# Turning results back on the vector engine, handing out stores and loads one by one, and reading transposed probabilities back on the scalar engine's queue

## The chip, the cores and the metric

The kernel runs on one core of a Trainium2 chip. The time is device microseconds from one launch, the median of several runs; a profile is one further execution, recorded by the hardware. The core has five engines that each work through their own list of instructions in order and wait for each other through semaphores: TensorE (PE), VectorE (DVE), ScalarE (ACT), GpSimd (POOL) and SyncE (SP). SP does no arithmetic here: it issues DMAs, in the order in which the program gives them.

## What is computed

Two blocks follow each other, for 8 batches, 576 rows and 512 columns:

```python
# attention, 8 heads of 64 columns, S = 576 rows
scores = scale * q @ k.T
kth    = the 32nd largest score of each row
attn   = softmax of the scores, those below kth left out
x      = attn @ v, heads side by side            # (8, 576, 512)
# mixer
u   = x + (x.T @ U @ V).T                        # rank 32, over the rows
out = u + relu(u @ w_ch1) @ w_ch2                # 512 -> 2048 -> 512
```

All tensors are float32 (parameters arrive in 64 bits and are narrowed on the chip).

## The kernel before

The work goes by *pairs* of heads (`g`, 32 of them, four to a batch) and, within a pair, by *chunks* of query rows (`t`): four of 128 rows that hold both heads side by side, and one of 64 rows per head, stacked. A *step* `n` is one chunk; 160 steps follow each other, and each step's code issues work of several chunks at different stages: scores of chunk n+1 (`scores`, L323), top-32 search of chunk n (`front`: MAX8 and MATCH_REPLACE8 on VectorE, L432 to L463, a fold of the row's two halves in `pair` with L390, L392, L393), masking (L488 on ScalarE, L491 on GpSimd) and exponential (L397) of chunk n or n-1, transposing of the probabilities of chunk n-1, and the product with v of chunk n-3 or so (`values`, L581, L585). The instructions are issued in the order in which the Python code calls them (a manual schedule); each engine runs its own in that order.

The probabilities must be transposed before the product with v. For most chunks (`shared`) VectorE does it in blocks of 32x32 (`blocks`, L518, into the buffer `y`), four DMAs on SP write `y` to DRAM (`away`, L524), and a fifth reads it back as `PT` (L528), so that the blocks land in their places. The last 64 columns are transposed on TensorE (L551) and copied by ScalarE (L552).

`load(g)` (L238) issues all loads of a pair on SP: for most pairs (`blocked`) 16 DMAs for q and k (L247, L252) and 5 for v (L276, L279, L280). `prep(g)` turns q and k with VectorE's 32x32 transpose (L293) at the end of chunk 1 of the pair before.

The MLP of a batch (`mlp`, L646) is a generator. It yields after each matmul, and `fill` (L748), called eight times in a step, takes as many matmuls from it as the ratio of the work asks for; so the MLP of one batch is spread over the attention of the next. The MLP has two parts by rows (320 and 256), each with 16 blocks of the first product (L656, a Relu on ScalarE, L668) and 4 column blocks of the second (L675). The result `oT` of a column block has columns in partitions. ScalarE copies it (L690), GpSimd adds u (L691), and it is *turned back*: `turned_back` (L696) makes a closure that `mlp` calls 13 matmuls later, or at once for the last block of a batch:

```python
                late.append(turned_back(b, chunks, lo, c, oT))
                yield w / C
        late.pop()()
```

For all batches but the last, the closure transposes with TensorE (L723, three or two transposes), copies with ScalarE (L725, L727) and stores with one or two DMAs (L729, L734). In the last batch all blocks but one are transposed by VectorE in 32x32 blocks (L705), and 12 or 8 DMAs (L710, L715) store the pieces where they belong. The last batch's MLP has no attention beside it.

Of the kernel before, what the change touches and what calls it, by code (L numbers as in the profile page):

```python
# [26 lines left out]
def kernel(  # L27
# [107 lines left out]
    def half(h):  # L135
        return slice(h * D, (h + 1) * D)
# [96 lines left out]

    raw, qkTs, S2s, uTs, XTs, dens = {}, {}, {}, {}, {}, {}
    probs, PTs, folds, fronts_of = {}, {}, {}, {}
    inverted = set()

    def load(g):  # L238
        b, h0 = g // NPAIR, 2 * (g % NPAIR)
        ld = loads.tile([P, 2 * S], F32, tag="ld", name="ld")  # L240
        if blocked(g):
            for i, src in enumerate((q, k)):
                for a in range(4):
                    ds = src[b, h0 + a // 2, :, a % 2 * BLK : (a % 2 + 1) * BLK]
                    to = ld[a * BLK : (a + 1) * BLK, i * S : (i + 1) * S]
                    lead = TAIL if i and a >= 2 else 0
                    nc.sync.dma_start(  # L247
                        to[:, lead : lead + MAIN].rearrange("i (t m d) -> i t m d", t=NT, d=BLK),
                        ds[0:MAIN].rearrange("(m i t) d -> i t m d", i=BLK, t=NT),
                    )  # L250
                    end = 0 if lead else MAIN
                    nc.sync.dma_start(  # L252
                        to[:, end : end + TAIL].rearrange("i (m d) -> i m d", d=BLK),
                        ds[MAIN:S].rearrange("(m i) d -> i m d", i=BLK),
                    )
            raw[g] = ld
        else:
            tiles = []
            ends = ld[:, 2 * MAIN : 2 * S].rearrange("p (h d) -> p h d", h=2)
            for j, src in enumerate((q, k)):  # L260
                t = ld[:, j * MAIN : (j + 1) * MAIN].rearrange("p (t h d) -> p t h d", t=NT, h=2)
                for i in range(2):
                    queue = nc.scalar if g == 0 and i else nc.sync
                    queue.dma_start(
                        t[:, :, i, :],
                        src[b, h0 + i, 0:MAIN, :].rearrange("(p t) d -> p t d", t=NT),
                    )
                tiles.append(t)
            for i, src in enumerate((q, k)):
                nc.sync.dma_start(  # L270
                    ends[half(i)], src[b, h0 : h0 + 2, MAIN:S, :].rearrange("h p d -> p h d")
                )
            raw[g] = tiles, ends
        va, vd, vt = (a[g % NV] for a in (vas, vds, vts))
        for i in range(2):
            nc.sync.dma_start(  # L276
                va[:, i], v[b, h0 + i, 0:MAIN, :].rearrange("(p t) d -> p t d", t=NT)
            )
            nc.sync.dma_start(vd[half(i), half(i)], v[b, h0 + i, MAIN:S, :])  # L279
        nc.sync.dma_start(vt[TAIL:P], v[b, h0 : h0 + 2, MAIN:S, :].rearrange("h p d -> p h d"))  # L280

    def blocked(g):

        return g > NPAIR
# [222 lines left out]
    def blocks(g, t):  # L509


        E2 = probs[g, t]
        PT = attn.tile([P, 2 * NT + 1, P], F32, tag="PT", name="PT")
        PTs[g, t] = PT
        y = attn.tile([P, 4, 2, NT, BLK], F32, tag="y", name="y", bufs=1)
        for h in (1, 0):
            a = h * (S + TAIL)
            nc.vector.transpose(  # L518
                y[:, :, h].rearrange("p r c j -> p c r j"),
                E2[:, a : a + MAIN].rearrange("p (c r j) -> p c r j", c=NT, r=4),  # L520
            )
        away = dram.tile([P, 4, 2 * P], F32, tag="away", name="away")
        for a in range(4):
            nc.sync.dma_start(  # L524
                away[:, a].rearrange("(r i) n -> i r n", r=4),
                y[a * BLK : (a + 1) * BLK].rearrange("i r h c j -> i r (h c j)"),
            )
        nc.sync.dma_start(  # L528
            PT[:, 0 : 2 * NT].rearrange("p a n -> p (a n)"), away.rearrange("p a n -> p (a n)")
        )  # L530

    def turns(g, t):

# [112 lines left out]
    def mlp(b):  # L646

        uT = uTs.pop(b)
        late = []
        for chunks, (lo, hi) in zip(PARTS, SPAN):  # L650
            w = hi - lo
            hTs = []
            for f in range(NF):
                ph = ps_m.tile([P, C], F32, tag="mm", name="mm")
                for cc in range(NC):
                    nc.tensor.matmul(  # L656
                        ph[:, 0:w],
                        lhsT=w1[:, cc, f * P : (f + 1) * P],
                        rhs=uT[:, cc, lo:hi],
                        start=(cc == 0),  # L660
                        stop=(cc == NC - 1),
                    )
                    if cc < NC - 1:
                        yield w / C
                if f % 2 == 0:
                    hT = mlpp.tile([P, 2, WIDE], F32, tag="hT", name="hT", bufs=HT)
                    hTs += [hT[:, 0], hT[:, 1]]
                nc.scalar.activation(hTs[f][:, 0:w], ph[:, 0:w], AF.Relu)  # L668
                if f == 4 and late:
                    late.pop()()  # L670
                yield w / C
            for c in range(NC):
                po = ps_m.tile([P, C], F32, tag="mm", name="mm")
                for f in range(NF):
# [4 lines left out]
                        start=(f == 0),  # L679
                        stop=(f == NF - 1),  # L680
                    )
                    if f == 12 and late:
                        late.pop()()
                    if f < NF - 1:
                        yield w / C
                oT = mlpp.tile([P, WIDE], F32, tag="oT", name="oT")
# [2 lines left out]
                else:  # L689
                    nc.scalar.copy(oT[:, 0:w], po[:, 0:w])  # L690
                    nc.gpsimd.tensor_tensor(oT[:, 0:w], oT[:, 0:w], uT[:, c, lo:hi], ALU.add)  # L691
                late.append(turned_back(b, chunks, lo, c, oT))
                yield w / C
        late.pop()()

    def turned_back(b, chunks, lo, c, oT):  # L696


        def run():
            cs = slice(c * P, (c + 1) * P)  # L700
            if b == B - 1 and (lo, c) != (SPAN[1][0], NC - 1):

                w = sum(rows(t) for t in chunks)
                ob = mlpp.tile([P, 3 * P], F32, tag="ob", name="ob", bufs=2)
                nc.vector.transpose(ob[:, 0:w], oT[:, 0:w])  # L705
                for a in range(4):
                    cs = slice(c * P + a * BLK, c * P + (a + 1) * BLK)
                    ba = ob[a * BLK : (a + 1) * BLK]
                    for t in chunks[0:2]:
                        nc.sync.dma_start(  # L710
                            out[b, 0:MAIN, cs].rearrange("(m i t) c -> t i m c", i=BLK, t=NT)[t],
                            ba[:, OFF[t] - lo : OFF[t] - lo + P].rearrange("i (m c) -> i m c", c=BLK),
                        )
                    if NT in chunks:
                        nc.sync.dma_start(  # L715
                            out[b, MAIN:S, cs].rearrange("(m i) c -> i m c", i=BLK),
                            ba[:, 2 * P : 2 * P + TAIL].rearrange("i (m c) -> i m c", c=BLK),
                        )
                return
            tp = ps_t.tile([P, 3, P], F32, tag="tp", name="tp")  # L720
            for i, t in enumerate(chunks):
                n = rows(t)
                nc.tensor.transpose(tp[0:n, i, :], oT[:, OFF[t] - lo : OFF[t] - lo + n], ident)  # L723
            ob = mlpp.tile([P, 3, P], F32, tag="ob", name="ob", bufs=2)
            nc.scalar.copy(ob[:, 0:2], tp[:, 0:2, :])  # L725
            if NT in chunks:
                nc.scalar.copy(ob[0:TAIL, 2], tp[0:TAIL, 2, :])  # L727
            t = chunks[0]
            nc.sync.dma_start(  # L729
                out[b, 0:MAIN, cs].rearrange("(p t) c -> p t c", t=NT)[:, t : t + 2, :],  # L730
                ob[:, 0:2],
            )
            if NT in chunks:
                nc.sync.dma_start(out[b, MAIN:S, cs], ob[0:TAIL, 2])  # L734

        return run

    MLP_WORK = 2 * NF * NC * S / C

# [5 lines left out]
    share = MLP_WORK / (NPAIR * SLOTS * (NT + SHORT))  # L745
    fillers, mixing, due = [], [], 0.0

    def fill(k=1):  # L748


        nonlocal due
        for _ in range(k):
            if passes:
                passes.pop(0)()
            if mixing and next(mixing[0], True):
                mixing.pop(0)
            due += share * (SHORT if t == NT else 1) * (EARLY if n <= 2 * ALONE + 2 else 1)
# [13 lines left out]
        if m % CH == NT:  # L771
            mixing.append(mixed(m // CH, 5, 1 if m < STEPS - 1 else 0))

    load(0)
    next_params(1)
    t = 0
    for _ in prep(0):
# [4 lines left out]
    for n in range(STEPS + 2):  # L782
        g, t = divmod(n, CH)
        if n < STEPS:
            if t == 0 and g + 1 < NP:
                load(g + 1)
            if t == 1 and g + 1 < NP:
                ready = prep(g + 1)
            fronts[n] = front(g, t)
            next(fronts[n])  # L790
# [79 lines left out]
        next(turning, None)  # L870
        if n > ALONE and (n - 1) % CH < NT:
            next(last, None)
        fill()
        next(turning, None)
        fill()
# [22 lines left out]
        fill(2)  # L898
    while mixing or fillers:
        fill()  # L900


# [29 lines left out]
```

## Time and profile before

| | |
|---|---|
| median of 3 runs | 1718.4 us (1717.51 to 1718.5) |
| the profiled execution | 1716.65 us, of which the span from first to last instruction is 1714.9 us |
| TensorE clock granted, mean | 0.970 |
| busy: TensorE matmul | 1613.5 us, 94% of the span |
| busy: VectorE | 1484.2 us, 87% |
| busy: ScalarE | 1023.3 us, 60% |
| busy: GpSimd | 944.9 us, 55% |
| DMA | 167.37 MB in 275837 packets, 98 GB/s; 173920 of the packets under 512 B |

A line of the profile names the source line, the engine, the operation and the program's names (written <- read). In the groups the count follows the x, then come the busy time in us and the mean in ns, then the time that the engine was idle before such an instruction, and what ended that wait. In a timeline the first number is the start in us. A float32 matmul appears as two records, a transpose as one. Matmuls overlap in TensorE's pipeline, so the mean of one is longer than the distance between two. A name with a q (SPq) is the engine's queue of instructions that it issues without computing, such as DMAs.

### The profile page before, as it was taken

To read this page: it belongs to the slowest core of one execution; us is meant where nothing else is said; L and a number is where in the kernel's file an instruction comes from. 1 tells how busy PE (TensorE), PEld (TensorE's weight loads), DVE (VectorE), ACT (ScalarE), POOL (GpSimd) and SP (SyncE) were. 2 spreads that over 40 slices of the span, in tenths; PEclk is the share of its full clock that TensorE was granted. 3 is DMA by queue.
4 is the path that set the end of the run, shared out by engine and by line. 5 is a ranking of instruction groups with operands and counts; after the bars stand their busy time and mean duration, and the time that the engine had idled before them with its cause. 6 is when DMAs were issued, how large, how long until landed. Compare 5 with 4: busy or idle time off the path is not lost.

```text
span 1714.9 us, 29637 instructions
## 1 busy us (share of the span) xinstructions
PE 1613.5 (94%) x9489; PEld 1219.8 (71%) x9489; DVE 1484.2 (87%) x4317; ACT 1023.3 (60%) x2582; POOL 944.9 (55%) x749
## 2 busy tenths in 40 slices
PE   4666799998999999999999999999999999999999
PEld 2444566787777877788677877788677877788777
DVE  7999989999999999999999999999999999992000
ACT  4888797665656556565656566565655566563100
POOL 4778578666555555565555555565555555552000
PEclk7777899999999999999999999999999999999999
DMA  3322322344444444444444444444444444432010
GB/s 87 95 84 84 84 78 61 77 123 122 108 112 112 117 117 106 112 116 114 115 109 111 119 112 108 114 113 114 111 108 120 118 108 114 106 93 71 3 16 13
DMA packets 275837, 167.37 MB, mean 98 GB/s; under 512 B 173920, under 2 KB 260192, under 8 KB 275680
## 3 DMA queue, kind: packets, MB, share of 16 engines
q1 hardware_dynamic: 274624, 165.20, 37.2%
q8 instruction: 75, 1.23, 0.3%
q14 instruction: 82, 0.67, 0.1%
q10 hardware_dynamic: 1056, 0.26, 0.1%
HBM read 101.42 MB, written 63.96 MB: 96 GB/s over the span
## 4 chain that ended last, share of the span: by engine, by line
PE 71%; DVE 19%; SPq 3%; ACT 2%; issue 2%; DMA 2%; POOL 1%; POOLq 0%; DVEq 0%; ACTq 0%
PE mm L656 27%; PE mm L675 21%; PE sc L323 8%; DVE upper L458 6%; PE O L585 6%; DVE m L463 6%; DVE first L446 2%; SPq L252 2%; PE tp L551 1%; PE O L571 1%; SPq L247 1%; PE up L631 1%; PE O L581 1%; PE tp L546 1%; DVE y L518 1%
## 5 line engine op out<-in xcount | busy, mean ns | idle before, releaser
L675 PE MATMUL mm<-hT,w 128*128 128x256 f32 (+1 forms) x2048 | 529.5, 407 | 0.0
L656 PE MATMUL mm<-uT,w 128*128 128x256 f32 (+1 forms) x2048 | 522.8, 407 | 0.0
L491 POOL TENSOR_TENSOR Ssb<-Ssb,E 128x576 f32<-128x576 f32 x271 | 379.2, 1417 | 246.2 <-ACT E L488 245.8
L656 PEld LDWEIGHTS mm<-uT,w 128*128 128x128 f32 x2048 | 380.0, 191 | 97.6 <-issue 2.6
L675 PEld LDWEIGHTS mm<-hT,w 128*128 128x128 f32 x2048 | 377.9, 191 | 93.0 <-issue 2.9
L463 DVE MAX8 m<-upper 128x8 f32<-128x304 f32 (+1 forms) x864 | 407.7, 508 | 3.6
L458 DVE MATCH_REPLACE8 upper<-m,upper 128x304 f32<-128x304 f32 (+1 forms) x576 | 285.7, 502 | 0.0
L390 POOL TENSOR_TENSOR lower<-Ssb 128x576 uint32<-128x576 uint32 (+1 forms) x135 | 174.3, 1291 | 147.2 <-ACT Ssb L351 51.0
L393 POOL TENSOR_TENSOR lower<-lower,upper 128x576 uint32<-128x576 uint32 (+1 forms) x135 | 174.3, 1291 | 112.2 <-DVE upper L392 104.7
L397 ACT ACTIVATE Ssb<-Ssb,nmax 128x576 f32<-128x576 f32 x286 | 221.5, 777 | 15.3 <-POOL Ssb L468 9.3
L668 ACT ACTIVATE hT<-mm 128x320 f32<-128x320 f32 (+1 forms) x256 | 105.1, 410 | 192.9 <-PE mm L656 191.0
L323 PE MATMUL sc<-qkT 64*128 64x288 f32 x1334 | 211.7, 441 | 8.6 <-ACT Ssb L358 7.8
L488 ACT ACTIVATE E<-Ssb,least 128x576 f32<-128x576 f32 x271 | 198.0, 769 | 5.2
L323 PEld LDWEIGHTS sc<-qkT 64*128 64x128 f32 x1334 | 116.3, 183 | 63.8 <-issue 24.2
L585 PE MATMUL O<-PT,va 128*64 128x128 f32 x2048 | 144.5, 285 | 3.3 <-DMA PT<-away 3.2
L518 DVE STREAM_TRANSPOSE y<-Ssb 128x512 f32<-128x512 f32 x208 | 134.5, 682 | 14.8 <-ACT Ssb L397 14.7
L351 ACT COPY Ssb<-sc 128x576 f32<-128x576 f32 x216 | 127.5, 643 | 32.6 <-PE sc L323 31.0
L688 DVE TENSOR_TENSOR oT<-uT,mm 128x320 f32<-128x320 f32 (+1 forms) x8 | 3.6, 454 | 144.5 <-PE mm L675 144.5
L585 PEld LDWEIGHTS O<-PT,va 128*64 128x64 f32 x2048 | 113.2, 140 | 19.7 <-DMA PT<-away 3.9
L432 DVE MAX8 upper<-lower 128x8 f32<-128x288 f32 x243 | 97.9, 439 | 23.2 <-POOL lower L393 21.2
L392 DVE TENSOR_TENSOR upper<-sc,Ssb 128x576 f32<-128x576 f32 (+1 forms) x135 | 92.0, 682 | 20.7 <-ACT Ssb L351 20.1
L458 DVE MATCH_REPLACE8 upper<-first,upper 128x304 f32<-128x304 f32 x243 | 109.8, 458 | 0.0
(91 smaller groups left out, 1878.7 us busy)
## 6 DMA issues: line engine op xcount, KB each, us to landing
away<-y SPq DMA_DIRECT2D x416, 128.0 KB, 2.4
PT<-away SPq DMA_DIRECT2D x104, 512.0 KB, 3.3
raw<-in_moe_w_ch_dram SPq DMA_DIRECT2D x32, 512.0 KB, 3.9
va<-in_v_dram SPq DMA_DIRECT2D x64, 128.0 KB, 2.2
out_dram<-ob SPq DMA_DIRECT2D x57, 128.0 KB, 2.0
ld<-in_q_dram SPq DMA_DIRECT2D x108, 64.0 KB, 2.6
ld<-in_k_dram SPq DMA_DIRECT2D x108, 64.0 KB, 2.3
ld<-in_q_dram SPq DMA_DIRECT2D x108, 8.0 KB, 2.2
```

Source lines behind the costliest of these rows:

```text
L323: nc.tensor.matmul(out, lhsT=qkT[half(h), 0, cols(t)], rhs=qkT[half(h), 1, lo:hi], start=True, stop=True,)
L390: nc.gpsimd.tensor_tensor(bottom, a.bitcast(U32), b.bitcast(U32), ALU.add)
L393: nc.gpsimd.tensor_tensor(bottom, bottom, top.bitcast(U32), ALU.subtract)
L397: nc.scalar.activation(E, chunk, AF.Exp, bias=nmax, scale=SCALE, accum_out=total)
L458: nc.vector.match_replace(nxt, ms[c], curs[c], NEG)
L463: nc.vector.max(ms[c], curs[c])
L488: nc.scalar.activation(gap, chunks[c], AF.Relu, bias=least[:, c : c + 1], scale=-WIDEN)
L491: nc.gpsimd.tensor_tensor(chunks[c], chunks[c], gap, ALU.subtract)
L518: nc.vector.transpose(y[:, :, h].rearrange("p r c j -> p c r j"), E2[:, a : a + MAIN].rearrange("p (c r j) -> p c r j", c=NT, r=4),)
L585: nc.tensor.matmul(O[half(h)], lhsT=va[:, h, j, :], rhs=PB[:, h, j] if shared(g, t) else PT[:, NT * h + j], start=False, stop=(j == NT - 1),)
L656: nc.tensor.matmul(ph[:, 0:w], lhsT=w1[:, cc, f * P : (f + 1) * P], rhs=uT[:, cc, lo:hi], start=(cc == 0), stop=(cc == NC - 1),)
L675: nc.tensor.matmul(po[:, 0:w], lhsT=w2[:, f, c * P : (c + 1) * P], rhs=hTs[f][:, 0:w], start=(f == 0), stop=(f == NF - 1),)
```

## The change

Four things change.

- `turned_back` becomes `turn_back`, and VectorE transposes every column block but the very last of the kernel. Nothing is called by the MLP's own counting any more: `later(6, job)` puts a job in a list, `tick()`, called after each MLP matmul, runs at most one job that is due. A turning back thus comes six MLP matmuls after its column block, also across the border of two batches.
- The 12 or 8 stores of a block are put in the same list, one for each of the next ticks (in the last batch they are issued at once).
- `load` becomes a generator that yields after each DMA. From pair 6 on, its DMAs are taken one by one by `fill` (`send`), starting at chunk 2 of the pair two before; the rest, if any, is sent at chunk 1.
- The readback of `away` into `PT` is taken out of `blocks` and put into `back`, which is called in the following step, behind the exponential `next(last, None)`, and issues it from ScalarE's queue.

```diff
@@ blocks
-        nc.sync.dma_start(
-            PT[:, 0 : 2 * NT].rearrange("p a n -> p (a n)"), away.rearrange("p a n -> p (a n)")
-        )
+        aways[g, t] = away
+
+    def back(g, t):
+
+        if (g, t) in aways:
+            nc.scalar.dma_start(
+                PTs[g, t][:, 0 : 2 * NT].rearrange("p a n -> p (a n)"),
+                aways.pop((g, t)).rearrange("p a n -> p (a n)"),
+            )
@@ mlp (after each matmul of both products)
+                    tick()
...
-                late.append(turned_back(b, chunks, lo, c, oT))
+                later(6, lambda a=(b, chunks, lo, c, oT): turn_back(*a))
                 yield w / C
-        late.pop()()
@@ turn_back
-            if b == B - 1 and (lo, c) != (SPAN[1][0], NC - 1):
+        if (b, lo, c) != (B - 1, SPAN[1][0], NC - 1):
+
+            w = sum(rows(t) for t in chunks)
+            ob = mlpp.tile([P, 3 * P], F32, tag="ob", name="ob", bufs=2)
+            nc.vector.transpose(ob[:, 0:w], oT[:, 0:w])
...
+                for to, piece in pieces:
+                    if b == B - 1:
+                        nc.sync.dma_start(to, piece)
+                    else:
+                        wait += 1
+                        later(wait, lambda to=to, piece=piece: nc.sync.dma_start(to, piece))
@@ new helpers
+    posts, ticks = [], 0
+
+    def later(wait, job):
+
+        at = ticks + wait
+        i = sum(p[0] <= at for p in posts)
+        posts.insert(i, (at, job))
+
+    def tick():
+
+        nonlocal ticks
+        ticks += 1
+        if posts and posts[0][0] <= ticks:
+            posts.pop(0)[1]()
+
+    coming = []
+
+    def send():
+
+        if coming and next(coming[0], True):
+            coming.pop(0)
@@ fill
+            send()
@@ the loop over the steps
-            if t == 0 and g + 1 < NP:
-                load(g + 1)
+            if t == 0 and g <= NPAIR:
+                for _ in load(g + 1):
+                    pass
+            if t == 2 and NPAIR <= g < NP - 2:
+                coming.append(load(g + 2))
             if t == 1 and g + 1 < NP:
+                while coming:
+                    send()
                 ready = prep(g + 1)
...
         if n > ALONE and (n - 1) % CH < NT:
             next(last, None)
+        back(*divmod(n - 2, CH))
         fill()
```

More of the change, by code (lines that the diff above doesn't have):

```diff
@@ L235 @@
     probs, PTs, folds, fronts_of = {}, {}, {}, {}
-    inverted = set()
+    inverted, aways = set(), {}
     def load(g):
@@ L241, in load @@
         if blocked(g):
+            raw[g] = ld
             for i, src in enumerate((q, k)):
@@ L250, in load @@
                     )
+                    yield
                     end = 0 if lead else MAIN
@@ L255, in load @@
                     )
-            raw[g] = ld
+                    yield
         else:
@@ L278, in load @@
             )
+            yield
             nc.sync.dma_start(vd[half(i), half(i)], v[b, h0 + i, MAIN:S, :])
+            yield
         nc.sync.dma_start(vt[TAIL:P], v[b, h0 : h0 + 2, MAIN:S, :].rearrange("h p d -> p h d"))
@@ L648, in mlp @@
         uT = uTs.pop(b)
-        late = []
         for chunks, (lo, hi) in zip(PARTS, SPAN):
@@ L668, in mlp @@
                 nc.scalar.activation(hTs[f][:, 0:w], ph[:, 0:w], AF.Relu)
-                if f == 4 and late:
-                    late.pop()()
                 yield w / C
@@ L681, in mlp @@
                     )
-                    if f == 12 and late:
-                        late.pop()()
+                    tick()
                     if f < NF - 1:
@@ L691, in mlp @@
                     nc.gpsimd.tensor_tensor(oT[:, 0:w], oT[:, 0:w], uT[:, c, lo:hi], ALU.add)
-                late.append(turned_back(b, chunks, lo, c, oT))
+                later(6, lambda a=(b, chunks, lo, c, oT): turn_back(*a))
                 yield w / C
[L694 to L700, printed above, removed]
-            if b == B - 1 and (lo, c) != (SPAN[1][0], NC - 1):
[L703 to L736, printed above, removed]
@@ new lines, in turn_back @@
+    def turn_back(b, chunks, lo, c, oT):
+        cs = slice(c * P, (c + 1) * P)
+        if (b, lo, c) != (B - 1, SPAN[1][0], NC - 1):
+            w = sum(rows(t) for t in chunks)
+            ob = mlpp.tile([P, 3 * P], F32, tag="ob", name="ob", bufs=2)
+            nc.vector.transpose(ob[:, 0:w], oT[:, 0:w])
+            wait = 0
+            for a in range(4):
+                cs = slice(c * P + a * BLK, c * P + (a + 1) * BLK)
+                ba = ob[a * BLK : (a + 1) * BLK]
+                pieces = [
+                    (
+                        out[b, 0:MAIN, cs].rearrange("(m i t) c -> t i m c", i=BLK, t=NT)[t],
+                        ba[:, OFF[t] - lo : OFF[t] - lo + P].rearrange("i (m c) -> i m c", c=BLK),
+                    )
+                    for t in chunks[0:2]
+                ]
+                if NT in chunks:
+                    pieces.append((
+                        out[b, MAIN:S, cs].rearrange("(m i) c -> i m c", i=BLK),
+                        ba[:, 2 * P : 2 * P + TAIL].rearrange("i (m c) -> i m c", c=BLK),
+                    ))
+                for to, piece in pieces:
[4 more added lines that the diff above has]
+                        later(wait, lambda to=to, piece=piece: nc.sync.dma_start(to, piece))
+            return
+        tp = ps_t.tile([P, 3, P], F32, tag="tp", name="tp")
+        for i, t in enumerate(chunks):
+            n = rows(t)
+            nc.tensor.transpose(tp[0:n, i, :], oT[:, OFF[t] - lo : OFF[t] - lo + n], ident)
+        ob = mlpp.tile([P, 3, P], F32, tag="ob", name="ob", bufs=2)
+        nc.scalar.copy(ob[:, 0:2], tp[:, 0:2, :])
+        t = chunks[0]
+        nc.sync.dma_start(
+            out[b, 0:MAIN, cs].rearrange("(p t) c -> p t c", t=NT)[:, t : t + 2, :],
+            ob[:, 0:2],
+        )
@@ L772, in weighted @@
             mixing.append(mixed(m // CH, 5, 1 if m < STEPS - 1 else 0))
-    load(0)
+    for _ in load(0):
+        pass
     next_params(1)
@@ L784 @@
         if n < STEPS:
-            if t == 0 and g + 1 < NP:
-                load(g + 1)
+            if t == 0 and g <= NPAIR:
+                for _ in load(g + 1):
+                    pass
+            if t == 2 and NPAIR <= g < NP - 2:
+                coming.append(load(g + 2))
             if t == 1 and g + 1 < NP:
+                while coming:
+                    send()
                 ready = prep(g + 1)
@@ L900 @@
         fill()
+    while posts:
+        tick()
 _INS = ['q', 'k', 'v', 'moe_U', 'moe_V', 'moe_w_ch1', 'moe_w_ch2']
```

## The prediction

> **What bounds the kernel now.** I first read the page's strip of 40 slices, to see where which engine is full.
>
> ```profile
> PE   4666799998999999999999999999999999999999
> DVE  7999989999999999999999999999999999992000
> ```
>
> Three stretches: up to about slice 6 (batch 0, no MLP yet) VectorE is full and TensorE is not; then both are at 90% or more; the last three slices are TensorE alone (the last batch's MLP). The change works in the middle one. Next the busy time of each engine over one whole batch there (start, end, length, then busy time and count of PE, PEld, DVE, ACT, POOL, clock, DMA share).
>
> ```profile
> 818.85:1012.61 193.76, 192.49 (x1161) 146.97 (x1161) 184.24 (x565) 118.32 (x304) 111.66 (x89) 1.00 0.44 113
> 1012.61:1206.37 193.76, 192.49 (x1161) 146.97 (x1161) 184.17 (x565) 118.33 (x304) 111.67 (x89) 1.00 0.44 112
> ```
>
> A batch repeats every 193.76 us to the hundredth, TensorE is idle 1.27 us of it, VectorE 9.6. So TensorE sets the pace: its MLP matmuls follow each other at 0.269 us (320 columns) and 0.216 us (256 columns) per record, the same as when it runs alone at the end, so its "busy" is work and not waiting. Where the 1.27 us are, and what a turning back costs, the timeline shows:
>
> ```profile
> 1205.94 0.44 PE L723 MATMUL tp<-ident,oT 128*128 128x128 f32 x2 [1.27 <-POOL oT L691]
> ```
> ```profile
> 1086.92 0.70 PE L675 MATMUL mm<-hT,w 128*128 128x320 f32 x2
> 1087.46 0.49 PE L723 MATMUL tp<-ident,oT 128*128 128x128 f32 x3
> 1087.79 0.43 PE L675 MATMUL mm<-hT,w 128*128 128x320 f32 x1
> ```
>
> Three transposes push the next matmul back by 1087.79 - 1087.46 = 0.33 us (0.11 each, far less than the mean in the next view). The one idle is at each batch's last column block, turned back the moment it is made, while GpSimd still adds the residual. The groups of instructions (busy us, mean ns | idle before, released by):
>
> ```profile
> L723 PE MATMUL tp<-ident,oT 128*128 128x128 f32 (+1 forms) x142 | 25.3, 276 | 10.3 <-POOL oT L691 9.8 <-DVE oT L688 0.5
> L725 ACT COPY ob<-tp 128x256 f32<-128x256 f32 x57 | 21.2, 372 | 127.2 <-PE tp L723 127.2
> L705 DVE STREAM_TRANSPOSE ob<-oT 128x320 f32<-128x320 f32 (+1 forms) x7 | 3.4, 483 | 0.7 <-DVE oT L688 0.3
> ```
>
> The last of these is the form that replaces the first two: 0.51 us at 320 columns, 0.445 at 256.
>
> [...]
>
> ```profile
> SPq L528 <- DMA away<-y: 205.9, 212, 3.1
> ```
>
> That is 206 us in 104 readbacks in which the sync queue stood behind its own writes. [...] here the 128-byte pieces of the last batch landed in 1.5 us (median), and DMA engines are 44% busy, so I charge nothing.
>
> **Part 1, turning back on VectorE.** Per batch TensorE loses 12 + 8 transposes: four groups of 0.33, three of 0.22 and one of 0.27, together 2.25 us, and the 1.27 us wait (the turning back now waits its six matmuls, on VectorE): 3.5 us of 193.76. ScalarE loses 8 copies of 0.37 and 4 of 0.26 (4 us) and the blockage in front of them (127 us in all, 18 a batch); none of this is on the path, it only makes what stands behind them earlier. VectorE gains 4 x 0.51 + 4 x 0.445 = 3.8 us: 184.2 to 188.0. Of its 9.6 us idle, 1.2 are gaps between instructions and 8.4 are six waits for things that TensorE's lateness delays (2.82 before L518, 1.66, 0.91 and 0.78 before L392, 1.29 and 0.52 before L432); these shrink as TensorE gets earlier. So VectorE needs 189.2 and TensorE 190.3: it fits, barely.
>
> New waits on VectorE: with L691's end against the time at which VectorE passes six matmuls later in the program's order, the 320-column blocks are ready 1.4 to 4.5 us early, but three of the four 256-column ones are late by 1.19, 1.60 and 1.18 us (VectorE runs ahead of TensorE there, and GpSimd adds late). Each such delay makes the next smaller: with their own work about 2.5 us at the end of the batch, which the 2.82 us wait that follows takes up. Behind them stand the MAX8s of the next step; the scores that wait for VectorE's L392 have 4.4 us or more in hand. I take 0.2 us per batch for this (bounds 0 and 2.5).
>
> **Part 2, readback from ScalarE's queue.** SP issues it today 3.8 us after the last transpose of y. The new place is behind the next step's first exponential (L397; for every fourth one behind L552). Against SP's issue ScalarE passes there 0.2 to 4 us later, so it hardly waits itself, but the data come later. The tight one is the third chunk of a pair:
>
> ```profile
> 1022.12 0.77 ACT L397 ACTIVATE Ssb<-Ssb,nmax 128x576 f32<-128x576 f32 x1
> ```
> ```profile
> 1025.67 1.09 PE L585 MATMUL O<-PT,va 128*64 128x128 f32 x16
> ```
>
> Issued between 1022.1 [...] and 1023.0, landing 3.3 us later (median; 3.0 to 5.4), it is there from 1025.4 to 1026.3, and TensorE wants it at 1025.67: between nothing and 0.6 us lost. The other three third chunks of a batch have 0.5 to 0.9 us more, the rest 4.5 to 7.8 between ScalarE's place and the use. I take 0.3 per batch (bounds 0 and 2). The issue itself, 0.34 us on SP, lies under the running exponential.
>
> **Part 3, stores and loads singly.** SP's work per batch: 80 stores x 0.475 us (spacing of L710) = 38, 84 loads x 0.64 = 54, 64 writes of y x 0.476 = 30: 122 of 191 us, no more than today with its waits. But it clusters. Between two writes of y that are 9.5 and then 8.6 us apart stand 8 loads and 8 stores, then 7 and 8: with the four writes 10.9 and 10.1 us of issuing, so the second write of y leaves 1.4 + 1.4 = 2.8 us late, and one more pair in the batch 1.7. The readback behind it, now at the head of ScalarE's queue, holds ScalarE by up to that, and a Relu behind it (L668) then frees TensorE's PSUM bank late; it has about 1.1 us in hand there. The PT itself has 6.5 - 3.3 = 3 us in hand. I take 0.7 us a batch (bounds 0 and 3). The loads now start four chunks ahead of their use instead of under two. I price that at nothing: today's last q/k load (issued 1039.6, 2.0 us to landing) is there 1.8 us before L293 reads it, and L293 has no idle before it (0.0); had that cover been gone, each late us would be VectorE's.
>
> **Sum.** 3.5 - 0.2 - 0.3 - 0.7 = 2.3 us per batch, for the six whose MLP runs beside a full TensorE (MLPs 1 to 6): 13.8. MLP 0 (236 to 430 us) has TensorE idle 10.8 us already and a wait of 2.3 us at the same place: I give it 1.5 (bounds -2 and 4). Together 15.3. The profiled execution took 1716.65 us (span 1714.9), so 1701.4; the median of the runs is 1.75 above it: **1703 us**.
>
> **Rivals.** *Full gain*: no new wait reaches TensorE; 7 x 3.5 = 24.5, less what MLP 0 does not give, 22 to 25: 1694 to 1696. For it: the margins above; against: both engines would stand above 98.7%. *VectorE becomes the bound*: the 8.4 us shrink little, since they end on ScalarE and GpSimd; then 3.8 us of new work eat most of the 3.5, and it ends at 0.3 to 1 us per batch: about 1713. For it: 95% busy, a 70 us stretch of each batch (1134 to 1206) with 0.13 us of waits, just where four turnings fall. *Slower*: SP's clusters. At ScalarE's readback the queue waits for writes of y that SP issues late; Relus and exponentials stand behind. It decides from 3.5 us of TensorE wait a batch; if three of the 16 readbacks are 1 us too late for TensorE (stores at the 0.63 us of the strided loads would do that) and part 2 is at its bound of 2, it loses 5, net 1.5 a batch: 1728. Against: 64% load of SP and its long pause before each pair's first chunk (18.8 us between writes). That the change does not do what it says can be left out: the order of the built program shows L723's transposes gone from all batches but one block.
>
> **How the numbers follow.** Forecast (1698 to 1709) 0.52; full gain (1691 to 1697) 0.13; VectorE-bound (1709 to 1717) 0.20, of which 0.13 below 1715; slower 0.15. A measurement tells 0.2%, 3.4 us, from no change: faster 0.52 + 0.13 + 0.13 = 0.78, same 0.08 (the rest of the third and a little of the last), slower 0.14. The range from 1691 to 1720 leaves out most of the slower case and little else.
>
> **What would show it.** Right: batch period about 191.5; L723 down to 2 and the 127 us before L725 gone; VectorE above 98% with the wait before L518 smaller; ACT's queue waiting for "away" by 1 to 4 us twice a batch; L585's wait for PT under 1 us a batch. Wrong: idle of L585 or L656 over 3 us a batch, L563 or the Relu waiting behind the readback, or DVE's new transposes waiting over 2 us a batch for oT.

## The result, and the profile after

The changed kernel takes 1747.7 us (median; 1744.5 to 1750.0) against 1718.45 us before: ratio 1.0172, interval 1.0159 to 1.0185. It is slower, where 1703 us was forecast with a range of 1691 to 1720. The profiled execution took 1749.97 us, its span is 1748.0 us against 1714.9.

Lines have moved: the first product of the MLP is now L666, its Relu L679, the second product L684, the writes of y L529, the readback L538, the product with v L596, VectorE's turning back L709, its stores L731.

First the groups that the forecast was about (columns as before):

```profile
L709 DVE STREAM_TRANSPOSE ob<-oT 128x320 f32<-128x320 f32 (+1 forms) x63 | 29.2, 464 | 35.4 <-POOL oT L699 35.1
...
L736 PE MATMUL tp<-ident,oT 128*128 128x128 f32 x2 | 0.4, 300 | 0.6 <-DVE oT L696 0.6
L738 ACT COPY ob<-tp 128x256 f32<-128x256 f32 x1 | 0.4, 372 | 28.3 <-PE tp L736 28.3
```

The change does what it says: 142 transposes on TensorE are down to 2, and 63 VectorE transposes are there where 7 were before. Of the 35.1 us in front of these, 30 lie after the end of the attention, where VectorE has nothing else to do; in a batch in the middle it is 0.4 us. Next, two whole batches (start, end, length, then busy time and count of PE, PEld, DVE, ACT, POOL, clock, DMA share, GB/s):

```profile
839.40:1036.47 197.07, 191.01 (x1142) 145.00 (x1140) 187.71 (x573) 114.94 (x293) 111.89 (x89) 1.00 0.45 111
1036.47:1235.62 199.15, 192.71 (x1142) 146.12 (x1141) 187.69 (x573) 115.05 (x293) 111.86 (x89) 0.99 0.44 110
```

A batch took 193.76 us before and takes 197 to 201 now. TensorE stands still for 6 us of it (1.27 before) and VectorE for 9 to 11; neither sets the pace by its work. From the starts of the MLPs: 8.6 us are lost up to the second MLP's start, then 7.2, 5.0, 3.3, 5.4 and 3.8 in the five following batches, and none after the start of the last batch's MLP. The waits (us in total, times, longest):

```profile
ACT hT L679 <- DMA away<-y: 38.4, 8, 5.4
...
PE mm L666 <- ACT hT L679: 23.2, 13, 4.6
...
PE O L596 <- DMA PT<-away: 13.9, 15, 2.1
...
ACT Ssb L402 <- DMA away<-y: 7.9, 5, 4.0
...
ACT oT L698 <- DMA away<-y: 7.7, 4, 2.4
```

The first and the last two are ScalarE standing behind the readback at the head of its queue, 54 us together; there was no such wait before. It reaches TensorE as late Relus (the second line); late PT (the third) holds TensorE as well. How one such wait comes about, the timeline of SP's queue shows (start, length):

```profile
733.70 1.77 SPq L529 DMA_DIRECT2D away<-y  x4
...
740.00 0.58 SPq L249 DMA_DIRECT2D ld<-in_k_dram  x1
742.04 0.32 SPq L255 DMA_DIRECT2D ld<-in_k_dram  x1
...
746.44 1.83 SPq L529 DMA_DIRECT2D away<-y  x4
...
756.96 1.82 SPq L529 DMA_DIRECT2D away<-y  x4
```

Between the writes stand 8 loads and 8 stores, then 7 and 8. VectorE's transposes into y for the last two of these writes:

```profile
742.30 1.28 DVE L523 STREAM_TRANSPOSE y<-Ssb 128x512 f32<-128x512 f32 x2
...
751.79 0.71 DVE L523 STREAM_TRANSPOSE y<-Ssb 128x512 f32<-128x512 f32 x1 [0.84 <-ACT Ssb L402]
```

So y was finished at 743.58 and 752.50, and the writes leave 2.86 and then 4.46 us late (here and below, "late" counts from the end of VectorE's last transpose into y to the start of the first write). And what hangs on the second:

```profile
755.87 3.62 PE L666 MATMUL mm<-uT,w 128*128 128x256 f32 x16
...
761.23 0.38 ACT L679 ACTIVATE hT<-mm 128x256 f32<-128x256 f32 x1 [4.55 <-DMA away<-y]
...
761.67 1.93 PE L666 MATMUL mm<-uT,w 128*128 128x256 f32 x5 [2.19 <-ACT hT L679]
```

ScalarE waits 4.55 us for the writes to land, issues the readback and does the Relu; TensorE, which needs that Relu to free a PSUM buffer, has stood 2.19 us. That is not all of the bill. The windows around it:

```profile
759.00:762.29 3.29, 1.10 (x6) 0.65 (x5) 3.29 (x10) 1.06 (x3) 1.42 (x1) 1.00 0.59 132
762.29:765.70 3.41, 3.41 (x10) 2.66 (x9) 3.41 (x14) 1.50 (x7) 0.00 (x0) 0.50 0.58 166
765.70:772.00 6.30, 6.30 (x48) 5.09 (x47) 4.54 (x16) 4.40 (x10) 4.33 (x4) 1.00 0.02 4
```

After the stall TensorE runs 3.41 us at half its clock (0.50). A budget over the whole run, from 200 us on, summed from the traces: TensorE's idle time is 21.5 us before and 55.2 after (+33.7); at half clock it works 8.9 us before and 27.1 after, and half of the difference is lost (+9.1); the transposes that are gone are worth 1.8 us in each of seven batches, as shown below (-12.6). The sum is +30.2, against +33.1 in the spans.

### The profile page after: what moved, and what is told of

Read it like the earlier page. It is cut to its first block, busy times and chain, and to the rows that moved or that the text cites. A ratio compares the mean times of both kernels' runs of the same rounds, so it can differ in the third digit from the quotient of the medians.

```text
span 1748.0 us, 29687 instructions
## 1 busy us (share of the span) xinstructions
PE 1613.0 (92%) x9349; PEld 1212.6 (69%) x9349; DVE 1509.6 (86%) x4373; ACT 1000.0 (57%) x2498; POOL 946.1 (54%) x749
## 4 chain that ended last, share of the span: by engine, by line
PE 56%; DVE 27%; DMA 7%; SPq 3%; POOL 3%; issue 2%; ACT 1%; ACTq 0%; DVEq 0%; POOLq 0%
PE mm L684 20%; PE mm L666 19%; DVE upper L463 9%; DVE m L468 8%; PE sc L328 6%; PE O L596 4%; DMA away<-y 3%; DVE first L451 3%; DMA PT<-away 2%; DVE y L523 2%; SPq L529 2%; DVE lower L439 1%; PE O L582 1%; DVE upper L437 1%; DVE upper L441 1%
## 5 line engine op out<-in xcount | busy, mean ns | idle before, releaser
L666 PE MATMUL mm<-uT,w 128*128 128x256 f32 (+1 forms) x2048 | 534.7, 413 | 28.3 <-ACT hT L679 23.2
L684 PE MATMUL mm<-hT,w 128*128 128x256 f32 (+1 forms) x2048 | 523.9, 407 | 0.0
L666 PEld LDWEIGHTS mm<-uT,w 128*128 128x128 f32 x2048 | 385.0, 194 | 135.3 <-ACT hT L679 29.4
L684 PEld LDWEIGHTS mm<-hT,w 128*128 128x128 f32 x2048 | 380.6, 191 | 96.7 <-issue 2.9
L679 ACT ACTIVATE hT<-mm 128x320 f32<-128x320 f32 (+1 forms) x256 | 104.6, 409 | 222.7 <-PE mm L666 182.8
L398 POOL TENSOR_TENSOR lower<-lower,upper 128x576 uint32<-128x576 uint32 (+1 forms) x135 | 174.1, 1290 | 99.5 <-DVE upper L397 91.8
L596 PE MATMUL O<-PT,va 128*64 128x128 f32 x2048 | 145.0, 285 | 14.0 <-DMA PT<-away 13.9
L596 PEld LDWEIGHTS O<-PT,va 128*64 128x64 f32 x2048 | 113.5, 141 | 31.5 <-DMA PT<-away 17.0
L605 ACT COPY XT<-O 128x128 f32<-128x128 f32 x128 | 34.2, 267 | 144.2 <-PE O L596 144.2
```

The source lines that it names most:

```text
L398: nc.gpsimd.tensor_tensor(bottom, bottom, top.bitcast(U32), ALU.subtract)
L596: nc.tensor.matmul(O[half(h)], lhsT=va[:, h, j, :], rhs=PB[:, h, j] if shared(g, t) else PT[:, NT * h + j], start=False, stop=(j == NT - 1),)
L666: nc.tensor.matmul(ph[:, 0:w], lhsT=w1[:, cc, f * P : (f + 1) * P], rhs=uT[:, cc, lo:hi], start=(cc == 0), stop=(cc == NC - 1),)
L684: nc.tensor.matmul(po[:, 0:w], lhsT=w2[:, f, c * P : (c + 1) * P], rhs=hTs[f][:, 0:w], start=(f == 0), stop=(f == NF - 1),)
```

## The experiments

The theory (T): single stores and single loads together fill SP's queue between two writes of y; the writes leave late, and with them all that waits for them. Rivals: VectorE's 3.8 us of new work set the pace (R1); the later place of the readback makes PT late by itself (R2); the single loads alone (R3). Three parts of the change can be undone one by one, and all eight combinations were run. Times are medians; the ratio is to the kernel before, run beside it (1717.3 to 1718.45 us).

| turned back by | loads | readback on | us | ratio, interval | run |
|---|---|---|---|---|---|
| TensorE | burst | SP | 1705.5 | 0.9931 (0.9914 to 0.9948) | e9 |
| TensorE | burst | ScalarE | 1706.8 | 0.9939 (0.9924 to 0.9953) | e6 |
| TensorE | single | SP | 1709.1 | 0.9953 (0.9938 to 0.9968) | e5 |
| TensorE | single | ScalarE | 1712.3 | 0.9971 (0.9961 to 0.9981) | e3 |
| VectorE | burst | SP | 1712.0 | 0.9971 (0.9964 to 0.9978) | e4 |
| VectorE | burst | ScalarE | 1706.6 | 0.9937 (0.9922 to 0.9951) | e2 |
| VectorE | single | SP | 1789.2 | 1.0416 (1.0400 to 1.0431) | e1 |
| VectorE | single | ScalarE | 1747.7 | 1.0172 (1.0159 to 1.0185) | the change |

All eight turn a block back six MLP matmuls after it is made; e9 differs from the kernel before in that alone. Where an average of the lateness is given, it is over the batches in the middle of the run (600 to 1400 us).

### e1, readback back on SP

```diff
-        aways[g, t] = away
+        nc.sync.dma_start(
+            PT[:, 0 : 2 * NT].rearrange("p a n -> p (a n)"), away.rearrange("p a n -> p (a n)")
+        )
```

> Changed kernel, but the readback of away is issued on SP straight behind the four writes, as before. Theory T (SP's stores and loads make the writes of y late, and the readback at the head of ScalarE's queue passes the lateness on to the Relus): the 55 us of ScalarE waiting for away are gone, TensorE's wait for hT (3 us a batch) falls below 0.5, its wait for PT stays between 0 and 2 us a batch because the writes are still late; 1705 to 1722 us. Rival R1 (VectorE's 3.8 us of new work a batch and its waits for oT set the pace): no change, 1742 to 1750. Rival R2 (the later place of the readback makes PT late): the PT wait is gone, the hT wait stays, about 1735.

Measured: 1789.2 us, 41.5 us slower than the change, where T expected a gain. ScalarE is no longer held and the hT wait is gone, as T said, but the wait for PT grew from 2 to 10 us a batch, and VectorE, which can't fill y again before the writes have read it, waits 36.4 us for late writes (6.2 in the change):

```profile
PE O L598 <- DMA PT<-away: 70.4, 27, 7.5
...
DVE y L523 <- DMA away<-y: 36.4, 11, 6.3
```

(L598 is here what L596 is in the change.) SP stands behind its own writes again, 203.6 us in all, about what it was in the kernel before, but now stores and loads pile up behind that: the fourth chunk's writes leave up to 7.9 us late (5.5 in the change). So ScalarE's being held, which I had put first, is not the root; the lateness is, and ScalarE's queue is the cheaper place for the readback once SP is full. Neither R1 nor R2 explains these 41.5 us: VectorE's work is that of the change, and the readback is back at its old place. Whether R1 holds for the change itself, e2 tells. One of the stalls with what follows it, in TensorE's timeline and as a window:

```profile
975.52 1.98 PE L598 MATMUL O<-PT,va 128*64 128x128 f32 x16 [5.18 <-DMA PT<-away]
```
```profile
972.66:979.49 6.83, 3.97 (x24) 2.75 (x24) 6.83 (x24) 0.91 (x2) 0.00 (x0) 0.50 0.51 141
```

The same 16 matmuls take 1.09 us in the kernel before and 1.98 here, at clock 0.50.

### e2, loads in a burst

```diff
-            if t == 0 and g <= NPAIR:
+            if t == 0 and g + 1 < NP:
                 for _ in load(g + 1):
                     pass
-            if t == 2 and NPAIR <= g < NP - 2:
-                coming.append(load(g + 2))
```

> Changed kernel, but all 21 loads of a pair go out at once at its predecessor's first chunk, as before; readback on ScalarE and single stores stay. T: between two writes of y stand at most 8 stores (3.8 us), so the writes leave less than 0.5 us late at chunks 2 and 3 and only the chunk behind the burst is late; ScalarE's waits fall from 55 to under 20 us, 1705 to 1722 us. R1: no change, 1742 to 1750. R2 (place): the 2 us of PT wait a batch stay, hT goes only in part, 1725 to 1740.

Measured: 1706.6 us. This one edit takes 41 us back, and R1 falls: VectorE does the same work as in the change. One batch and the waits for the writes:

```profile
816.61:1007.97 191.36, 190.47 (x1141) 145.15 (x1140) 186.70 (x573) 115.57 (x293) 111.77 (x89) 1.00 0.47 114
```
```profile
ACT x L623 <- DMA away<-y: 33.4, 18, 3.1
...
ACT hT L679 <- DMA away<-y: 4.5, 3, 2.0
```

The batch is 191.4 us, the 191.5 of the forecast. Late are now the writes of a pair's first chunk, behind the burst (2.2 us on average, 4.0 at most); there ScalarE is held in front of L623, mostly not in front of a Relu, and TensorE's idle time is 0.3 to 2.3 us a batch. Against the change the span is 45.1 us shorter: TensorE's idle time falls from 55.2 to 21.7 us, and its work at half clock from 27.1 to 9.9, of which half counts (8.6): together 42.1.

### e3, TensorE turns back

```diff
-        if (b, lo, c) != (B - 1, SPAN[1][0], NC - 1):
+        if b == B - 1 and (lo, c) != (SPAN[1][0], NC - 1):
```

and the copy and store of the last 64 rows as before.

> Changed kernel, but TensorE turns the results back and one or two whole stores follow, as before; single loads and readback on ScalarE stay. T: without the 80 small stores a batch SP has 8 loads (5.1 us) and one or two stores between two writes 9 us apart, so none leaves more than 0.5 us late; ScalarE does not wait for away; TensorE has its 2.25 us of transposes back: 1714 to 1724 us. R1: VectorE has its 3.8 us back as well, 1714 to 1724 (this run does not tell T from R1). R2 (place): the PT wait stays, 1726 to 1738. A rival R3 (the single loads alone, by their early DMA traffic): stays above 1735.

Measured: 1712.3 us, a little better than T's interval. Writes leave at most 1.1 us late (from the second MLP on), and ScalarE waits for them once, for 0.8 us. R2 and R3 fall: single loads and late readback stand here together, and no batch from the third MLP on has more than 1.4 us of TensorE idle.

### e4, VectorE and its stores alone

The edits of e1 and e2 together.

> Only the first part of the change: VectorE turns back, stores dealt out singly, but the loads in one burst and the readback on SP behind the writes as before. T: TensorE keeps the relief of 3.5 us a batch, no wait of ScalarE for away, PT waits under 1 us a batch: 1697 to 1710 us. R1 (VectorE): 1725 to 1748. If SP's stores delay the writes even without the loads, PT waits of 1 to 2 us a batch: 1708 to 1718.

Measured: 1712.0 us, in the third of the expected ranges. With the readback on SP the first chunk's writes, behind the burst, leave 4.4 us late on average; TensorE is idle 1 to 4 us a batch, and 16.1 us in all are waits for PT. Moving the readback to ScalarE's queue is worth 5.4 us here (e2).

### e5 and e6, one part alone

The edit of e3 with that of e1 (single loads alone), and with that of e2 (readback alone).

> Only the single loads: TensorE turns back with one or two whole stores, the readback is on SP behind the writes. T: 8 loads (5.1 us) and the readback's wait of about 2 us stand between two writes 9 to 10 us apart, which just fits; writes at most 1 us late, PT wait 0 to 1.5 us a batch: 1715 to 1727 us. If the loads alone were the cause of the slowdown (R3), 1735 or more.

> Only the readback on ScalarE's queue: TensorE turns back, loads in one burst. T: nothing makes the writes late but the burst, in front of the first chunk of a pair, where there is time: 1710 to 1718 us. R2 (the later place by itself makes PT late by up to 2 us a batch): 1724 to 1732.

Measured: 1709.1 and 1706.8 us, both better than expected; I had left out that TensorE's earlier turning back stays in them. Alone, the loads make the fourth chunk's writes 1.4 us late on average (2.1 at most there) and cost 3.7 us against e9, all of it in the first two MLPs; the readback's later place costs 1.3 us, less than the intervals can tell apart. Their batches in the middle, 192.27 us, are those of e9 to the hundredth.

### e7, the late place on SP's queue

```diff
-            nc.scalar.dma_start(
+            nc.sync.dma_start(
                 PTs[g, t][:, 0 : 2 * NT].rearrange("p a n -> p (a n)"),
```

> Changed kernel with the readback at its new, late place, but issued by SP instead of ScalarE. T: the writes are as late as in the changed kernel (4.5 to 5.5 us at the fourth chunk), ScalarE is not held, so TensorE's wait for hT (3 us a batch) is gone, its wait for PT grows to 3 to 6 us a batch: 1735 to 1755 us. If only the hold of ScalarE costs time and lateness itself does not, 1715 to 1725.

Measured: 1777.5 us (ratio 1.0345, 1.0329 to 1.0361), worse than either theory gave. The writes are as late as in the change (2.5 us on average at the fourth chunk, 2.4 in the change), but the readback now stands in SP's order behind further stores and loads and leaves up to 10.3 us after y:

```profile
PE O L596 <- DMA PT<-away: 53.8, 16, 5.3
```

So with a full SP, what is issued in front of the readback is paid by TensorE. This run differs from the change in the queue alone: ScalarE's, hold included, saves 30 us.

### e8, a quarter of the stores

```diff
-                    else:
+                    elif a == 0:
                         wait += 1
                         later(wait, lambda to=to, piece=piece: nc.sync.dma_start(to, piece))
```

> Changed kernel, but of the 12 or 8 stores of a block only those of the first 32 columns are issued in the first seven batches (3 or 2; three quarters of the output of these batches stay unwritten). VectorE's work, the single loads and ScalarE's readback stay. T: SP's two full windows shrink by 6 stores of 0.475 us each, no write is late, TensorE keeps its relief: 1698 to 1706 us. R1 (VectorE): 1735 or more.

Measured: 1706.5 us (0.9937, 0.9920 to 0.9953), just above T's interval; the writes leave at most 0.8 us late (from the second MLP on). So taking 60 of 80 stores from a batch does the same as bunching the loads (e2): it needs both to fill the windows.

### e9, only the time of turning back

The edits of e1, e2 and e3 together.

> All three parts undone; of the change only the timing of the turning back is left: TensorE turns each block back six MLP matmuls after it is made (before: 13, or at once for a batch's last block). The missing corner of the table of parts. If the kernels with TensorE's turning back (1707 to 1712 us) owe their gain to this timing (the 1.27 us a batch of waiting for oT is gone, seven times, 9 us): 1705 to 1711. If they owe it to loads and readback: 1715 to 1719.

Measured: 1705.5 us. The gain of all the kernels with TensorE's turning back is this: a block is turned back six matmuls after it is made and never at once. (Before, it was 13 matmuls for six of a batch's eight blocks, 20 for the last block of the first part, and at once for the last of the batch.) A batch of it:

```profile
813.02:1005.30 192.28, 192.28 (x1162) 147.37 (x1161) 184.33 (x565) 118.54 (x305) 111.70 (x89) 1.00 0.44 114
```

TensorE has no idle time left, and 192.28 - 190.47 (e2) = 1.8 us is what the twenty transposes of a batch cost it.

### e10 and e11, loads single but elsewhere or thinner

```diff
-            if t == 2 and NPAIR <= g < NP - 2:
+            if t == 4 and NPAIR <= g < NP - 2:
```
```diff
-        if coming and next(coming[0], True):
+        turn[0] += 1
+        if coming and (all or turn[0] % 3) and next(coming[0], True):
```

> Changed kernel, but the single loads of a pair start at the fifth chunk instead of the third, so that 13 of 21 fall into the long pause of SP's writes. T (stores, loads and the wait of SP for the readback fill two windows of 9 us one after the other, the second inherits the first one's lateness): only one full window is left, writes at most 3 us late there and nothing inherited; 1704 to 1718 us. If the number of DMAs on SP alone mattered and not where they stand: 1740 or more.

> Changed kernel, but a load goes out in two of three places only (5.3 instead of 8 between two writes, all else as in the changed kernel). T: each full window shrinks by 1.7 us, so its lateness falls from 2.9 and 4.5 to about 1.1 and 1.5 us; ScalarE's waits for away fall under 15 us in all: 1706 to 1720 us. If lateness is not the cause, 1740 or more.

Measured: 1710.8 us (0.9962, 0.9947 to 0.9977) and 1710.2 us (0.9957, 0.9943 to 0.9972), both as T expected. The DMAs are the same in number; what counts is how many stand between two writes. In e11 the fourth chunk's writes still leave up to 3.25 us late (in e10 3.7, and 4.4 once at 447 us), more than the 1.5 expected, but that is under the 4.5 to 5.5 of the change, and TensorE's waits shrink more than in proportion (e11):

```profile
ACT hT L679 <- DMA away<-y: 26.6, 10, 3.4
...
PE O L596 <- DMA PT<-away: 8.4, 10, 2.4
```

ScalarE still waits 38 us in all (T expected under 15), yet TensorE is idle about 1 to 2.5 us a batch, not 6. So about 3 us of lateness seem to be in hand, and what goes beyond that is paid.

### e12, a version that beats both

The edit of e2, and TensorE turns back in the first batch (with its copy and store of the last 64 rows); VectorE from the second on, readback on ScalarE.

```diff
-        if (b, lo, c) != (B - 1, SPAN[1][0], NC - 1):
+        if b > 0 and (b, lo, c) != (B - 1, SPAN[1][0], NC - 1):
```

> Loads in one burst, readback on ScalarE, VectorE turns back from the second batch on; the first batch's MLP, beside which VectorE is full and TensorE waits, is turned back by TensorE. If VectorE is the bound there (with VectorE turning back, the second MLP started at 433.3 us, with TensorE at 428.1), this keeps 5 us and the shorter batches: 1700 to 1704 us, below both kernels. If not, 1706 to 1708.

Measured: 1699.0 us, ratio 0.9892 (0.9877 to 0.9906). The first MLP's stretch, in e2 and in e12:

```profile
236.00:433.26 197.26, 184.40 (x1122) 139.45 (x1121) 184.69 (x560) 130.30 (x319) 132.13 (x104) 0.97 0.37 92
```
```profile
236.00:427.58 191.58, 184.16 (x1140) 140.22 (x1138) 180.32 (x546) 133.72 (x330) 131.94 (x104) 0.98 0.36 93
```

TensorE does 184 us of work in both; VectorE 4.4 us more in e2, and the stretch is 5.7 us longer. That is 5.7 of the 7.6 us between the two runs. In the middle of the stretch TensorE has time to spare in e2 and VectorE has none (e2, then e12):

```profile
320.00:410.00 90.00, 85.21 (x549) 68.10 (x548) 89.45 (x276) 53.77 (x139) 53.12 (x42) 1.00 0.47 115
```
```profile
320.00:410.00 90.00, 87.49 (x558) 70.19 (x557) 89.41 (x277) 55.33 (x142) 52.59 (x42) 0.98 0.45 116
```

With VectorE's turning back, e12 takes the small stores of that batch away too, but they are not the reason: with a quarter of them (e8) the second MLP starts at 434.5 us, with TensorE turning back beside the same loads and readback (e3) at 430.2.

### e13, readback on GpSimd

The lateness was larger than my sum of issue times, and the trace of the change shows SP standing 1.4 us at 740.6 until the readback issued at 738.37 had landed. In the program and in the trace the DMAs of SP and ScalarE share eight semaphores, and each waits until the DMA that had its semaphore before it has landed: of the 1810 DMAs in that trace that have such a predecessor, none was issued before it had landed, the nearest 0.02 us after. Theory L, in the expectation, is that these waits are what the sum left out.

```diff
-            nc.scalar.dma_start(
+            nc.gpsimd.dma_start(
                 PTs[g, t][:, 0 : 2 * NT].rearrange("p a n -> p (a n)"),
```

> Changed kernel with the readback issued by GpSimd instead of ScalarE, at the same place of the program. In the program the DMAs of SP and ScalarE take eight semaphores in turn, so that each waits until the eighth DMA before it has landed, a readback among them; GpSimd's DMAs have semaphores of their own. Theory L (SP's waits for the readback to land, about 2 us in a full window, are what the prediction's sum left out): without them the writes of y leave 0.5 to 1 us late at the third chunk and 2 to 3 us at the fourth instead of 2.9 and 4.5 to 5.5; with ScalarE free of the hold as well, 1708 to 1730 us unless GpSimd is held instead. Rival (the issuing alone fills the windows): lateness stays above 4 us at the fourth chunk, 1735 or more.

Measured: 1751.9 us (1.0205, 1.0185 to 1.0225). As the whole explanation Theory L falls: SP's waits for the readback are gone from the trace, but where the fourth chunk's writes are late, they still leave 3.1 to 5.8 us late (4.5 to 5.5 in the change). It is not empty: in every second of these pairs the third chunk's writes are now 0.1 to 0.2 us late, 1.4 to 1.8 in the change. The time of this run doesn't tell what the waits cost, since GpSimd in its turn comes late with the fold (second line below, 14.0 us in the change), and PT later still (first line, 13.9 in the change):

```profile
PE O L596 <- DMA PT<-away: 51.0, 34, 5.4
...
DVE upper L437 <- POOL lower L398: 43.1, 44, 4.3
```

## Why the prediction was wrong

**The step that failed is part 3, "I take 0.7 us a batch for this" (bounds 0 and 3).** e2 gives the term by itself: the single loads, beside the single stores, cost 41 us, 2 to 8 us in each of seven batches, 5.9 on average. The place was named rightly (SP between the writes, the readback at the head of ScalarE's queue, the Relu behind it); the size went wrong in three ways.

- *The windows were mis-sized.* A write leaves late by what SP takes from one write to the next beyond the time by which the ends of y lie apart, and lateness adds up: what the first window leaves, the second inherits. The windows of the pair shown above were put at 10.9 and 10.1 us; SP took 12.7 and 10.5, of which 1.4 and 0.2 were waits for the readback to land, which the sum did not have. y ended 9.9 and 8.9 us apart there, no closer than the 9.5 and 8.6 of the forecast. In the other late pair of a batch stand 8 loads and 6 stores, then 7 and 7, by the same spacings 9.9 and 9.7 us; SP took 11.3 and 11.4. And there y came closer: it ended 12.45 and 7.90 us apart before (616.77, 629.22, 637.12) and 9.85 and 7.38 after (636.37, 646.22, 653.60). The slack had been VectorE's wait before L518, and part 1 itself said that this wait would shrink:

```profile
DVE y L518 <- ACT Ssb L397: 14.7, 7, 2.8
```
```profile
628.51 0.71 DVE L518 STREAM_TRANSPOSE y<-Ssb 128x512 f32<-128x512 f32 x1 [2.81 <-ACT Ssb L397]
```
```profile
DVE y L523 <- ACT Ssb L402: 14.9, 29, 0.9
```

(All waits before, one of them in the timeline, all waits after: the one long wait a batch is gone.) So I took away a wait in one part and used it as cover in another. Predicted were 1.4 and 2.8 us in one pair and 1.7 in the other; measured are 2.1 to 3.3 and 4.5 to 5.1 in the one, 1.4 to 1.8 and 5.0 to 5.5 in the other.
- *The price of lateness is not linear.* The 3 us that PT was given in hand agree with e11. The 1.1 us of the Relu no run measures by itself; in the stall shown above 4.55 us of ScalarE's waiting became 2.19 of TensorE's. With at most 3.3 or 3.7 us of lateness in the middle batches little is lost (e11, e10: 3.6 and 4.2 us more than e2), with 4.5 to 5.5 us it is 41.
- *A TensorE stall was priced at its own length.* Of the 33 us, 9.1 are matmuls at half clock.

**The rival "SP's clusters" is what happened**, from its cause to its marks (idle of L666 3.3 us a batch, 23.2 in seven, where over 3 was named; the Relu behind the readback). I gave it 1728 us and little chance, since SP's load of 64% and its long pause spoke against it. A mean load says nothing of a window of 9 us, and the pause does not lie where loads and stores meet.

**Part 1, TensorE's relief of 3.5 us a batch**: right in kind. The wait of 1.27 us is gone; e9, which has only the new time of turning back, gains 12 us (seven such waits would be 8.9). The twenty transposes cost 1.8 us, not 2.25. Two readings were off without bearing on the result: VectorE's six waits sum to 8.0 us, not 8.4, and of the 127 us before L725 28 belong to the very last block, which stays on TensorE (L738 above).

**VectorE's new waits for oT, 0.2 us a batch**: 0.4 us, right. Its new work, 3.8 us: 187.7 - 184.2 = 3.5. In the middle batches it fits (e2: 191.4 us); that both engines stand above 98.7% was not reached (TensorE 99.5%, VectorE 97.6%). For MLP 0 I gave a gain of 1.5 us: there the second rival holds, with VectorE as the bound (e12); its turning back costs 5.5 us there (433.3 against 427.8 us at the second MLP's start, e2 and e9). This is why e2 ends at 1706.6 us and no lower than e9, and why e12 is better than both.

**Part 2, 0.3 us a batch for the readback's place**: alone it is 1.3 us in the whole run (e6 against e9), which fits, though the intervals can't tell it from nothing. That the issue can come as early as part 2 allowed for, while ScalarE still computes, is measured: 76 of the 104 readbacks of the change were issued up to 0.7 us before the end of the instruction in front of them. The forecast gave the second queue no gain of its own, which was my estimate. Where SP has room, none was measured (e6 against e9: 1.3 us slower); where it has none, ScalarE's queue is worth 29.8 us (e7 against the change).

**What stays open**: a part of SP's time. In 18 full windows of the change, from 636 to 1452 us, SP took 24.8 us more than the forecast's spacings of stores, loads and writes give. 16.8 of these are waits for a readback to land; in the first windows with 8 loads and 6 stores they are all of it. The cause of the other 8.0 us is not known, and e13, without these waits, still has 0.1 to 1.7 us too much in such windows.

## What to carry to other kernels

Work handed to a queue "one at a time" was cheap here where the queue had room between the issues that others wait for (single loads beside whole stores: 3.7 us, e5 against e9, and 5.5 us, e3 against e6) and cost 41 us where it had none (beside single stores: the change against e2): count the DMAs between two urgent ones, and use the spacing that the change will leave, not the one it finds. When a change adds a second stream to the same queue, price both together, and lay bulk issues into the long pause. And look at when a job is done before moving it to another engine: doing it six matmuls later, on the same engine, was worth 12 us here; all else in the best version (e12) is worth 6.5.

## What the runs showed of the hardware

TensorE's half-clock stretches came after its idle times. From 210 us to 100 us before the end, the trace of the kernel before has one stretch at clock 0.50 and that of the change has six, of 3.41 us (3) or 6.83 us (4); each begins 2.0 to 3.3 us after the start of a TensorE idle time, and these idle times were 2.06 to 4.62 us long. Of the idle times of 0.4 to 1.5 us in the two traces none of 33 was followed by one, of those of 1.5 to 2.5 us 4 of 12, of those above 2.5 us all 3 (2.77, 3.78 and 4.62 us). What such a stretch costs on top of the stall I estimate as half of TensorE's work in it: after the 2.19 us shown with the result 1.7 us (it works all of the 3.41 us), after the 5.18 us of e1 2.0 us (it works 3.97 of the 6.83 us).
